# Local attention scores from a reordered key buffer: one product of 160 columns in place of products of 128 and 32

## The chip, the cores and the metric

The kernel runs on one core of a Trainium2 chip. A core has TensorE (PE in the profile, its weight loads are PEld), which multiplies matrices into PSUM; VectorE (DVE), ScalarE (ACT) and GpSimd (POOL), which work on elements; SyncE (SP), which here only issues DMAs; and 16 DMA engines. Each engine runs its own instructions in order and waits on semaphores for the others. The metric is the device time of one execution in microseconds (us), the median of several runs.

## The reference

The first half is attention with 32 global and 512 local tokens in each of 8 batches and 8 heads of 64 dimensions. The second half, a routed layer of eight experts over the 4352 tokens that come out, is not touched by the change.

```python
s_g = scale * np.matmul(q_g, k_all.transpose(0, 1, 3, 2))          # global queries, all keys
out_g = np.matmul(sm(s_g), v_all)
s_ll = scale * np.matmul(q_l, k_l.transpose(0, 1, 3, 2))
mask = np.abs(pos[:, None] - pos[None, :]) <= window               # window = 32
s_ll = np.where(mask, s_ll, -1000000000.0)
s_lg = scale * np.matmul(q_l, k_g.transpose(0, 1, 3, 2))           # local queries, global keys
out_l = np.matmul(sm(np.concatenate([s_lg, s_ll], axis=-1)), np.concatenate([v_g, v_l], axis=2))
```

So a local query sees the 32 global keys and the local keys at most 32 places away.

## The kernel before

**Tiling.** A unit n = 4b + hp is one batch b and one pair hp of heads; there are 32 units. The 512 local queries of a unit are cut into 8 blocks of 64. A block of both heads makes 128 rows; it needs 128 local keys (64 of its own, 32 on either side) and the 32 global ones, 160 scores in a row. Units 0 to 5 use a plainer form with the two heads in separate products (line 334); the change leaves that form alone.

**The loop** (lines 516 to 634) runs steps s = 0 to 33. The order of work on each engine is the order in which the program text issues it; nothing is rescheduled. Step s does, among other things:

- `st_B(s, 0..2)`: the scores of unit s in three parts of 3, 3 and 2 blocks. For each block, line 337 multiplies the queries `qbd` with 128 contiguous columns of the key buffer `kTe`, and line 339 multiplies the same queries with the 32 columns of `kgT`. VectorE then adds the mask and takes the maximum (L344), and ScalarE the exponentials into `Pu` (L347).
- `st_G1` in even steps: scores of the global queries of two units against all keys (L407), in rounds of four products, of 480, 32 and 32 columns; one call for each half g of a batch. `st_G2` and `st_G3` in odd steps finish them; the last product of `st_G3` (L433) reads `vgn`, the global values.
- `st_D1(s-1)`, `st_D2`: transposes of the exponentials (L354, L368) and of finished rows (L364), with their copies out of PSUM (L356, L370, L372).
- `st_A(s+1)`: transposes of the next unit's keys and queries (L305). VectorE copies the keys to `kTe` (L307), ScalarE the queries to `qbd` (L314, two copies).
- `st_E(s-1)`: the products with the values (L388). They read `va` and `vb` (local values in two alignments) and `vgz` (global values spread over the rows).
- from step 5 on, pieces of the first two experts fill the rest of TensorE's time: `p_l1` (L475, four products) and `p_l2` (L489, eight). They share two PSUM buffers, `ps_mm`, in turn, so a piece can start when the piece before last has been copied out: `p_l1` by ScalarE or VectorE (`hT`, L478 or L480), `p_l2` by ScalarE (`yst`, L492).

In a step the pieces come in the order p_l1, p_l2, p_l1, p_l1, p_l2, p_l1; where one step's last p_l1 is followed by the next step's first, the profile shows eight L475 in one row.

**Loads.** GpSimd issues the loads of q, k, v and of weights in its own order, through `queue`. SyncE issues `vgz` (L161) and `vgn` (L162) from a small DRAM copy `vg16`, and from batch 2 on three DMAs (L191 to L193) that move `va` into `vb`; in batches 0 and 1 GpSimd's copies do that (`part`). `clear_z` fills `vgz` and `vgn` once for each of their two buffers, on GpSimd. The results of `p_l2` are stored by SyncE, too (L496).

Of the kernel before, what the change touches and what calls it, by code (L numbers as in the profile page):

```python
# [18 lines left out]
NEG = -8.0e9  # L19
# [4 lines left out]
def kernel(  # L24
# [31 lines left out]
    KW = P  # L56
    SW = KW + Sg
    VW = Dh + 1
    assert (B, H, Sl, Dh, Sg) == (8, 8, 512, 64, 32) and D == H * Dh and F % P == 0
    scale = 1.0 / float(Dh) ** 0.5  # L60

# [66 lines left out]
    with ExitStack() as att:  # L128
# [5 lines left out]
        ps_po = att.enter_context(tc.tile_pool(name="ps_po", bufs=1, space=PSUM))  # L134

        qpl = [att_c.tile([P, Sl], FP16, name=f"qpl{i}") for i in range(2)]
        mask = att_c.tile([P, 3, SW], FP32)
        kgT = att_c.tile([P, HP, B * Sg], FP16)
        qgT = att_c.tile([P, HP, B * Sg], FP16)
        qbd = [att_c.tile([P, NHB, P], FP16, name=f"qbd{i}") for i in range(2)]  # L140
        kTe = [att_c.tile([P, W + Sl + W], FP16, name=f"kTe{i}") for i in range(4)]
        vgr = [att_c.tile([P, 4 * H * VW], FP16, name=f"vgz{i}") for i in range(2)]
        vgz = [t.rearrange("p (a h v) -> p a h v", a=4, h=H) for t in vgr]
        vgn = [att_c.tile([P, H, VW], FP16, name=f"vgn{i}") for i in range(2)]
        own = att_c.tile([P, 4], FP16)
# [13 lines left out]
        def load_vz(b):  # L159
            for i in range(4):  # L160
                nc.sync.dma_start(out=vgz[b % 2][i:P:4, i, :, 0:Dh], in_=vg16[b])  # L161
            nc.sync.dma_start(out=vgn[b % 2][P - Sg : P, :, 0:Dh], in_=vg16[b])  # L162

        def load_v(b):
            va, vb = vab[b % 2]
            vz = vgz[b % 2]
            src = v_l[b].rearrange("h s d -> s h d")

            def first():
                nc.gpsimd.dma_start(out=vg16[b], in_=v_g[b].rearrange("h g d -> g h d"))  # L170
                nc.gpsimd.dma_start(out=va[W:P, 0, :, 0:Dh], in_=src[0:96])

            def mid(j):
                nc.gpsimd.dma_start(out=va[:, j, :, 0:Dh], in_=src[P * j - W : P * j + 96])  # L174

            def last():
                nc.gpsimd.dma_start(out=vb[HB : HB + W, NJ - 1, :, 0:Dh], in_=src[Sl - W : Sl])

            def part(eng, lo):
                if lo:  # L180
                    eng.tensor_copy(out=vb[96:P, NJ - 1], in_=va[W : 2 * W, 0])
                    eng.tensor_copy(out=vb[0:HB, 0:2], in_=va[HB:P, 0:2])
                    eng.tensor_copy(out=vb[0:HB, 2:NJ], in_=va[HB:P, 2:NJ])
                else:
                    eng.tensor_copy(out=vb[HB:P, 0:2], in_=va[0:HB, 1:3])
                    eng.tensor_copy(out=vb[HB:P, 2], in_=va[0:HB, 3])

            def move():
                if b < 2:
# [4 lines left out]
                if b > 1:  # L194
                    load_vz(b)

            return [first] + [lambda j=j: mid(j) for j in range(1, NJ)] + [last, move]

# [61 lines left out]
        nc.scalar.activation(out=ones_f[:, 0:1], in_=ones_f[:, 0:1], func=AF.Exp, scale=0.0)  # L260
        nc.vector.memset(mask, 0.0)
        for t in (kTe[0], kTe[2], kTe[3]):
            nc.vector.memset(t[:, 0:W], 0.0)
            nc.vector.memset(t[:, W + Sl :], 0.0)

        def clear(i, eng):
            va, vb = vab[i]
# [22 lines left out]
        run(steps)  # L290
        clear_z(0, nc.gpsimd)
        load_vz(0)

        st = {}
        NPL = 6

        def st_A(n):
            b, hp = divmod(n, HP)
            qs, ks = staged[b]
            qb, kt = qbd[n % 2], kTe[n % 4]  # L300
            pt = [ps_tr.tile([P, Sl], FP16, tag="tr", name="pk"), ps_sc.tile([P, Sl], FP16, tag="sc", name="pq")]
            for t, src in enumerate((ks, qs)):
                for so in range(NJ):
                    for a in range(2):
                        nc.tensor.transpose(pt[t][HB * a : HB * (a + 1), P * so : P * (so + 1)],  # L305
                                            src[:, 2 * hp + a, so, :], identity)
            nc.vector.tensor_copy(out=kt[:, W : W + Sl].rearrange("c (p s) -> c p s", s=NJ),  # L307
                                  in_=pt[0].rearrange("c (s p) -> c p s", s=NJ))
            if n < NPL:
                nc.scalar.copy(out=qpl[n % 2].rearrange("c (p s) -> c p s", s=NJ), in_=pt[1].rearrange("c (s p) -> c p s", s=NJ))  # L310
                return
            for a in range(2):
                r = slice(HB * a, HB * (a + 1))
                nc.scalar.copy(out=qb[r, :, HB * a : HB * (a + 1)].rearrange("c i (p s) -> c i p s", s=NJ),  # L314
                               in_=pt[1][r].rearrange("c (s i p) -> c i p s", s=NJ, i=NHB))

        def st_B(n, part):
# [10 lines left out]
            for ii in range(ni):  # L328
                i = i0 + ii
                if n < NPL:  # L330
                    for c0, c1, kk in ((0, KW, kt[:, HB * i : HB * i + KW]), (KW, SW, kgT[:, hp, Sg * b : Sg * (b + 1)])):
                        for a in range(2):
                            r = slice(HB * a, HB * (a + 1))
                            nc.tensor.matmul(sc[r, SW * ii + c0 : SW * ii + c1], qpl[n % 2][r, HB * i : HB * (i + 1)],
                                             kk[r], start=True, stop=True)
                    continue
                nc.tensor.matmul(sc[:, SW * ii : SW * ii + KW], qb[:, i, :],  # L337
                                 kt[:, HB * i : HB * i + KW], start=True, stop=True)
                nc.tensor.matmul(sc[:, SW * ii + KW : SW * (ii + 1)], qb[:, i, :],
                                 kgT[:, hp, Sg * b : Sg * (b + 1)], start=True, stop=True)  # L340
            for ii in range(ni):
                i = i0 + ii
                mi = 0 if i == 0 else (2 if i == NHB - 1 else 1)
# [54 lines left out]
        def st_G1(b, g):  # L398
            n0 = HP * b + 2 * g
            gc = slice(Sg * b, Sg * (b + 1))  # L400
            sg = ps_po.tile([P, 2 * 512], FP32, tag="po")
            for c0, c1, k0 in ((0, Sl - W, 2 * W), (Sl - W, Sl, W), (Sl, S, None)):
                for hh in range(4):
                    pr, a = divmod(hh, 2)
                    r = slice(HB * a, HB * (a + 1))
                    rhs = kgT[r, 2 * g + pr, gc] if k0 is None else kTe[(n0 + pr) % 4][r, k0 : k0 + c1 - c0]
                    nc.tensor.matmul(sg[W * hh : W * (hh + 1), c0:c1], qgT[r, 2 * g + pr, gc], rhs, start=True, stop=True)  # L407
            m2 = att_wk.tile([P, 2], FP32, tag="m2")
            nc.vector.reduce_max(out=m2[:, 0:1], in_=sg[:, 0:S], axis=AX.X)
# [15 lines left out]
        def st_G3(b, g):  # L425
# [3 lines left out]
            for t in range(5):  # L429
                for par in range(2):  # L430
                    r, h0 = slice(HB * par, HB * (par + 1)), 4 * g + 2 * par
                    rhs = vb[:, t, h0 : h0 + 2, :] if t < NJ else vgn[b % 2][:, h0 : h0 + 2, :]
# [657 lines left out]
```

## Time and profile before

| what | value |
|---|---|
| median of 3 runs | 998.58 us (998.53 to 999.15) |
| the profiled execution's own time | 998.93 us |
| its span, first to last instruction | 997.2 us |
| granted TensorE clock over the span | 0.998 |
| TensorE busy | 982.5 us (99%) |
| VectorE busy | 767.2 us (77%) |
| ScalarE busy | 655.5 us (66%) |
| GpSimd busy | 301.7 us (30%) |
| line 337, 208 products of 128 columns | 27.6 us busy, 217 ns each |
| line 339, 208 products of 32 columns | 24.5 us busy, 178 ns each |
| line 307, 32 key copies on VectorE | 22.0 us busy, 687 ns each |
| line 314, 52 query copies on ScalarE | 32.5 us busy, 624 ns each |

The durations of products overlap, since a product starts while earlier ones still drain; so 217 and 178 ns are not what a product costs when others follow, and start times have to be compared instead. A line of the timeline gives the start, the duration, the engine, the line of the kernel, the operation, output and inputs, their shapes and how many instructions were merged; in brackets stands the idle time before it and what ended it. "Columns" of a product are those of its moving operand.

### The profile page before, as it was taken

Reading aid. Unit: us, or ns where it says so; the run is one execution under the profiler, and the core shown is the slowest. Engines: PE = TensorE matmul, PEld = TensorE weight load, DVE = VectorE, ACT = ScalarE, POOL = GpSimd, SP = SyncE. Lnnn points to the kernel's source line nnn. Section 1 sums busy time; section 2 is a strip of 40 time slices with the busy share of each in tenths; the row PEclk is TensorE's granted clock in tenths of the full one; section 3 lists DMA queues with packets and bytes.
Section 4 is the critical chain, followed back from the end, with each engine's and each line's share of the span. In section 5 each row is a group of like instructions: output and inputs, shape, how many; then the busy total and the mean of one; then the engine's idle time right before and its main releaser. Section 6 shows DMA issues by size and latency. Waiting matters only on the chain.

```text
span 997.2 us, 22451 instructions
## 1 busy us (share of the span) xinstructions
PE 982.5 (99%) x8868; PEld 641.0 (64%) x8868; DVE 767.2 (77%) x1858; ACT 655.5 (66%) x1342; POOL 301.7 (30%) x364
## 2 busy tenths in 40 slices
PE   7899999999999999999999999999999999999998
PEld 4566566656665555666666666676767676776764
DVE  7866665666653755889999888997899999888885
ACT  6888888888884566765555555557765555555551
POOL 9748887888850102111111111111111111100000
PEclk9999999999999999999999999999999999999999
DMA  9999999999952387554543333575664543123043
GB/s 167 186 156 199 239 206 221 222 200 222 234 144 85 108 241 169 161 147 121 122 107 74 75 75 74 128 214 129 165 148 117 117 96 66 53 65 74 2 106 127
DMA packets 138058, 138.68 MB, mean 139 GB/s; under 512 B 56608, under 2 KB 110048, under 8 KB 135904
## 3 DMA queue, kind: packets, MB, share of 16 engines
q0 software_dynamic: 105696, 87.32, 49.6%
q1 hardware_dynamic: 31696, 49.60, 15.5%
q8 instruction: 69, 1.13, 0.5%
q10 hardware_dynamic: 560, 0.33, 0.1%
q14 instruction: 37, 0.30, 0.1%
HBM read 144.46 MB, written 39.58 MB: 185 GB/s over the span
## 4 chain that ended last, share of the span: by engine, by line
PE 94%; POOL 3%; DMA 1%; DVE 1%; issue 0%; SPq 0%; ACT 0%; POOLq 0%; DVEq 0%
PE z L810 30%; PE pa L908 18%; PE py L489 12%; PE ph L475 12%; PE pb L908 9%; PE pc L908 4%; PE po L388 1%; PE ptw L354 1%; PE zp L879 1%; PE sc L337 1%; DMA vgz<-vg 1%; PE pk L305 1%; PE tgx L364 1%; PE pq L305 1%; PE sg L407 0%; POOL va L174 0%
## 5 line engine op out<-in xcount | busy, mean ns | idle before, releaser
L810 PEld LDWEIGHTS <-hs 128*128 128x128 f16 x2264 | 220.7, 98 | 91.8 <-DVE hs L806 0.4
L810 PE MATMUL z<-w2e,hs 128*128 128x256 f16 x1304 | 195.6, 273 | 0.0
L810 PE MATMUL z<-v,hs 128*128 128x256 f16 x960 | 144.0, 273 | 0.0
L475 PE MATMUL ph<-xT,w1e 128*128 128x512 f16 (+1 forms) x576 | 129.3, 367 | 0.6 <-ACT xT L372 0.6
L347 ACT ACTIVATE Pu<-ms,mx 128x160 f16<-128x160 f32 x256 | 120.1, 636 | 13.3 <-DVE mx L344 10.4
L489 PE MATMUL py<-w2e,hT 128*128 128x512 f16 x544 | 128.2, 379 | 0.0
L831 ACT COPY z<-z 128x256 f32<-128x256 f32 x98 | 35.0, 357 | 141.7 <-PE z L810 141.7
L908 PEld LDWEIGHTS <-w1e 128*128 128x128 f16 x960 | 87.1, 98 | 51.6 <-issue 1.0
L908 PE MATMUL pa<-t,s 128*128 128x512 f16 x384 | 114.2, 379 | 0.0
L726 POOL DMA_DIRECT2D w1e<-in_moe_w_dram x24 | 17.5, 734 | 297.5 <-PE pa L908 220.4
L344 DVE CUSTOM_DVE_ANT_0 ms<-sc,mask 128x160 f32<-128x160 f32 x256 | 70.2, 320 | 46.6 <-ACT yst L492 30.0
L844 DVE SCALAR_TENSOR_TENSOR oy<-z,lg,oy 128x512 f32<-128x512 f32 x128 | 95.8, 749 | 7.6 <-ACT oy L849 5.1
L806 DVE TENSOR_TENSOR hs<-hs 128x512 f16<-128x512 f16 x224 | 94.9, 424 | 8.2
L912 DVE CUSTOM_DVE_ANT_0 hx<-pb,s 128x512 f16<-128x512 f32 x96 | 65.9, 687 | 36.4 <-ACT s L942 30.2
L726 POOL DMA_DIRECT2D w2e<-in_moe_w_dram x24 | 19.8, 833 | 243.6 <-PE z L810 214.2
L928 ACT ACTIVATE hs<-pa 128x512 f16<-128x512 f32 x96 | 57.2, 596 | 47.0 <-PE pa L908 46.9
L475 PEld LDWEIGHTS <-w1e 128*128 128x128 f16 x576 | 53.4, 98 | 52.9
L912 DVE CUSTOM_DVE_ANT_0 hs<-pb,s 128x512 f16<-128x512 f32 x96 | 65.9, 686 | 24.1 <-ACT s L942 23.7
L908 PEld LDWEIGHTS <-s 128*128 128x128 f16 x720 | 65.6, 98 | 28.5 <-issue 0.3
L489 PEld LDWEIGHTS <-hT 128*128 128x128 f16 x544 | 49.8, 98 | 51.9
L480 DVE TENSOR_SCALAR hT<-ph 128x512 f16<-128x512 f32 x58 | 40.1, 692 | 55.1 <-PE ph L475 55.0
L478 ACT ACTIVATE hT<-ph 128x512 f16<-128x512 f32 (+1 forms) x86 | 50.6, 588 | 28.8 <-PE ph L475 28.4
(197 smaller groups left out, 1971.0 us busy)
## 6 DMA issues: line engine op xcount, KB each, us to landing
ys<-yd SPq DMA_DIRECT2D x68, 256.0 KB, 3.2
yd<-yst SPq DMA_DIRECT2D x16, 1024.0 KB, 5.9
pw<-in_moe_w_dram POOLq DMA_DIRECT2D x24, 512.0 KB, 10.1
kept<-psum POOLq DMA_DIRECT2D x24, 512.0 KB, 5.3
s<-kept POOLq DMA_DIRECT2D x12, 768.0 KB, 8.9
v<-kept POOLq DMA_DIRECT2D x12, 768.0 KB, 8.9
w1e<-in_moe_w_dram POOLq DMA_DIRECT2D x12, 512.0 KB, 5.3
w2e<-in_moe_w_dram POOLq DMA_DIRECT2D x12, 512.0 KB, 6.7
```

What stands on the lines that cost most here:

```text
L344: nc.vector.tensor_tensor_reduce(out=ms[:, ii, :], in0=sc[:, SW * ii : SW * (ii + 1)], in1=mask[:, mi, :], scale=-scale, scalar=BIG, op0=A ...
L347: nc.scalar.activation(out=d["Pu"][:, i // 4, :, i % 4], in_=ms[:, ii, :], func=AF.Exp, scale=-1.0, bias=d["mx"][:, i : i + 1])
L475: nc.tensor.matmul(ph[:, 0:n], wts[e][0][:, dk, P * fm : P * (fm + 1)], xT[:, dk, c0 : c0 + n], start=(dk == 0), stop=(dk == DP - 1))
L478: nc.scalar.activation(out=hT[:, fm, 0:n], in_=ph[:, 0:n], func=AF.Relu)
L480: nc.vector.tensor_scalar(out=hT[:, fm, 0:n], in0=ph[:, 0:n], scalar1=0.0, scalar2=None, op0=ALU.max)
L489: nc.tensor.matmul(py, hT[:, fk, P * c : P * (c + 1)], wts[e][1][:, fk, :], start=(fk == 0), stop=(fk == FT - 1))
L806: nc.vector.tensor_tensor(out=o, in0=x, in1=y, op=op)
L810: nc.tensor.matmul(o, lhs[:, fk, :], rhs[:, fk, :], start=(first and fk == 0), stop=(fk == HF - 1), skip_group_check=True)
L844: nc.vector.scalar_tensor_tensor(out=o, in0=z, scalar=p, in1=o, op0=ALU.mult, op1=ALU.add)
L908: nc.tensor.matmul(o, lhs[:, dk, P * f : P * (f + 1)], rhs[:, dk], start=(first and n == 0 and dk == 0), stop=(dk == HD - 1), skip_group_c ...
L912: nc.vector._custom_dve(TENSOR_ADD_SAT, out=self.to(i, j), in0=self.of(ps), in1=self.of(s), s0=BIG, s1=0.0)
L928: nc.scalar.activation(out=self.to(1, 0), in_=self.of(self.pa), func=AF.Relu)
```

## The change

It gives each key buffer `kTe` 24 pieces of 32 columns in place of 18. From unit 6 on, the keys lie in them in an order in which every fifth piece from piece 8 on holds the 32 global keys, written by a new ScalarE copy (`k_global`), and the local pieces lie such that each block's 160 keys can be read in one go: an odd block reads 160 contiguous columns, an even one five pieces of 32 that lie 64 columns apart. So the two products of a block become one. The copy of the local keys by VectorE becomes three copies.

In an odd block the keys then stand in another order, pieces 0, 2, 1, 3 as it were. From batch 2 on, the values `vb` are laid out in the same order (five moves by SyncE in place of three, the same bytes) and two permuted masks are made, in step 7. In batch 1 (`natural`), whose `vb` GpSimd fills in the old order, odd blocks keep two products and read the local keys through a permuted access pattern. `st_G1` reads its local keys in one round of 512 columns from batch 2 on, and in four of 128 in batch 1's second half.

`vgn` gets one buffer in place of two. Its load leaves `load_vz`: batch 0's stands behind the first `load_vz`, the others are issued at the start of step 4b + 2. GpSimd's fills of the second buffer go. A small tile of the routing part, `dg`, takes a buffer of the tag `ms`.

```diff
+    KC = 24
-        mask = att_c.tile([P, 3, SW], FP32)
+        mask = att_c.tile([P, 4, SW], FP32)
-        kTe = [att_c.tile([P, W + Sl + W], FP16, name=f"kTe{i}") for i in range(4)]
+        kTe = [att_c.tile([P, KC * W], FP16, name=f"kTe{i}") for i in range(4)]
-        vgn = [att_c.tile([P, H, VW], FP16, name=f"vgn{i}") for i in range(2)]
+        vgn = att_c.tile([P, H, VW], FP16)
+        def natural(b):
+            return b < 2
+        def k_block(n, i):
+            kt, r = kTe[n % 4], i // 2 * 5 * W
+            if i % 2:
+                return kt[:, r + 4 * W : r + 9 * W]
+            return kt[:, r : r + 9 * W].rearrange("c (k w) -> c k w", w=W)[:, 0:9:2]
+        def k_natural(n, i):
+            r = (i // 2 * 5 + 4) * W
+            return kTe[n % 4][:, r : r + 4 * W].rearrange("c (y x w) -> c x y w", x=2, w=W)
+        def k_global(n):
+            b, hp = divmod(n, HP)
+            kg = kTe[n % 4][:, 4 * W : 24 * W].rearrange("c (r k w) -> c r k w", k=5, w=W)[:, :, 4]
+            nc.scalar.copy(out=kg, in_=kgT[:, hp, Sg * b : Sg * (b + 1)].unsqueeze(1).to_broadcast([P, NJ, Sg]))
...
-            nc.sync.dma_start(out=vgn[b % 2][P - Sg : P, :, 0:Dh], in_=vg16[b])
...
-                nc.sync.dma_start(out=vb[0:HB, :], in_=va[HB:P, :])
-                nc.sync.dma_start(out=vb[HB:P, 0 : NJ - 1], in_=va[0:HB, 1:NJ])
+                nc.sync.dma_start(out=vb[0:W, :], in_=va[HB : HB + W, :])
+                nc.sync.dma_start(out=vb[HB : HB + W, :], in_=va[HB + W : P, :])
+                nc.sync.dma_start(out=vb[W:HB, 0 : NJ - 1], in_=va[0:W, 1:NJ])
+                nc.sync.dma_start(out=vb[HB + W : P, 0 : NJ - 1], in_=va[W:HB, 1:NJ])
...
-            eng.memset(vgn[i][0 : P - Sg], 0.0)
-            eng.memset(vgn[i][P - Sg : P, :, Dh:VW], 1.0)
+            if i == 0:
+                eng.memset(vgn[0 : P - Sg], 0.0)
+                eng.memset(vgn[P - Sg : P, :, Dh:VW], 1.0)
...
@@ st_A, from unit 6 on @@
+            ko = pt[0].rearrange("c (s r h o p) -> c o r h p s", s=NJ, r=4, h=2, o=2)
+            for o in range(2):
+                kd = kt[:, (2 + 2 * o) * W : (22 + 2 * o) * W].rearrange("c (r k p s) -> c r k p s", r=4, k=5, s=NJ)
+                kd = kd[:, :, 0:2] if o else kd[:, :, 0:5:4]
+                nc.vector.tensor_copy(out=kd, in_=ko[:, o])
+            nc.vector.tensor_copy(out=kt[:, 22 * W : 23 * W].rearrange("c (p s) -> c p s", s=NJ), in_=ko[:, 0, 0, 0])
+            k_global(n)
...
@@ st_B @@
-                nc.tensor.matmul(sc[:, SW * ii : SW * ii + KW], qb[:, i, :],
-                                 kt[:, HB * i : HB * i + KW], start=True, stop=True)
-                nc.tensor.matmul(sc[:, SW * ii + KW : SW * (ii + 1)], qb[:, i, :],
-                                 kgT[:, hp, Sg * b : Sg * (b + 1)], start=True, stop=True)
+                elif natural(b) and i % 2:
+                    nc.tensor.matmul(sc[:, SW * ii : SW * ii + KW], qb[:, i, :], k_natural(n, i), start=True, stop=True)
+                    nc.tensor.matmul(sc[:, SW * ii + KW : SW * (ii + 1)], qb[:, i, :],
+                                     kgT[:, hp, Sg * b : Sg * (b + 1)], start=True, stop=True)
+                else:
+                    nc.tensor.matmul(sc[:, SW * ii : SW * (ii + 1)], qb[:, i, :], k_block(n, i), start=True, stop=True)
...
@@ st_G1 @@
-            for c0, c1, k0 in ((0, Sl - W, 2 * W), (Sl - W, Sl, W), (Sl, S, None)):
+            if n0 < NPL:
+                cols = [(0, Sl - W, 2 * W), (Sl - W, Sl, W)]
+            elif natural(b):
+                cols = [(P * t, P * (t + 1), 2 * t + 1) for t in range(NJ)]
+            else:
+                cols = [(0, Sl, None)]
+            for c0, c1, k0 in cols + [(Sl, S, None)]:
...
+        def permuted_masks():
+            for i in (3, 2):
+                nc.vector.tensor_copy(out=mask[:, i, 0:KW].rearrange("q (y x w) -> q x y w", x=2, w=W),
+                                      in_=mask[:, 1, 0:KW].rearrange("q (x y w) -> q x y w", x=2, w=W))
+            nc.vector.memset(mask[:, 2, 3 * W : KW], NEG)
...
+            if 4 < s < NU and hp == 2:
+                nc.sync.dma_start(out=vgn[P - Sg : P, :, 0:Dh], in_=vg16[b])
...
+            if s == 7:
+                permuted_masks()
...
-            dg = att_wk.tile([P, P], FP32, tag="dg", bufs=1)
+            dg = att_wk.tile([P, 3, SW], FP32, tag="ms", name="dg")[:, 0, 0:P]
```

The masks are made behind `st_G3n` of step 7 and ahead of that step's last `p_l1`, whose copy out of PSUM is VectorE's (L480).

More of the change, by code (lines that the diff above doesn't have):

```diff
@@ L176, in last @@
             def last():
-                nc.gpsimd.dma_start(out=vb[HB : HB + W, NJ - 1, :, 0:Dh], in_=src[Sl - W : Sl])
+                r = HB if natural(b) else W
+                nc.gpsimd.dma_start(out=vb[r : r + W, NJ - 1, :, 0:Dh], in_=src[Sl - W : Sl])
             def part(eng, lo):
@@ L188, in move @@
             def move():
-                if b < 2:
+                if natural(b):
                     return part
                 nc.sync.dma_start(out=vb[96:P, NJ - 1], in_=va[W : 2 * W, 0])
-                nc.sync.dma_start(out=vb[0:HB, :], in_=va[HB:P, :])
-                nc.sync.dma_start(out=vb[HB:P, 0 : NJ - 1], in_=va[0:HB, 1:NJ])
-                if b > 1:
-                    load_vz(b)
+                nc.sync.dma_start(out=vb[0:W, :], in_=va[HB : HB + W, :])
+                nc.sync.dma_start(out=vb[HB : HB + W, :], in_=va[HB + W : P, :])
+                nc.sync.dma_start(out=vb[W:HB, 0 : NJ - 1], in_=va[0:W, 1:NJ])
+                nc.sync.dma_start(out=vb[HB + W : P, 0 : NJ - 1], in_=va[W:HB, 1:NJ])
+                load_vz(b)
             return [first] + [lambda j=j: mid(j) for j in range(1, NJ)] + [last, move]
@@ L262 @@
         for t in (kTe[0], kTe[2], kTe[3]):
-            nc.vector.memset(t[:, 0:W], 0.0)
-            nc.vector.memset(t[:, W + Sl :], 0.0)
+            nc.vector.memset(t[:, 0 : W], 0.0)
+            nc.vector.memset(t[:, W + Sl : 2 * W + Sl], 0.0)
         def clear(i, eng):
@@ L292 @@
         load_vz(0)
+        nc.sync.dma_start(out=vgn[P - Sg : P, :, 0:Dh], in_=vg16[0])
         st = {}
@@ L306, in st_A @@
                                             src[:, 2 * hp + a, so, :], identity)
-            nc.vector.tensor_copy(out=kt[:, W : W + Sl].rearrange("c (p s) -> c p s", s=NJ),
-                                  in_=pt[0].rearrange("c (s p) -> c p s", s=NJ))
+            kp = kt[:, W : W + Sl].rearrange("c (p s) -> c p s", s=NJ)
             if n < NPL:
+                nc.vector.tensor_copy(out=kp, in_=pt[0].rearrange("c (s p) -> c p s", s=NJ))
                 nc.scalar.copy(out=qpl[n % 2].rearrange("c (p s) -> c p s", s=NJ), in_=pt[1].rearrange("c (s p) -> c p s", s=NJ))
                 return
+            ko = pt[0].rearrange("c (s r h o p) -> c o r h p s", s=NJ, r=4, h=2, o=2)
[5 more added lines that the diff above has]
+            k_global(n)
             for a in range(2):
@@ L335, in st_B @@
                                              kk[r], start=True, stop=True)
-                    continue
-                nc.tensor.matmul(sc[:, SW * ii : SW * ii + KW], qb[:, i, :],
-                                 kt[:, HB * i : HB * i + KW], start=True, stop=True)
-                nc.tensor.matmul(sc[:, SW * ii + KW : SW * (ii + 1)], qb[:, i, :],
-                                 kgT[:, hp, Sg * b : Sg * (b + 1)], start=True, stop=True)
+                elif natural(b) and i % 2:
[4 more added lines that the diff above has]
+                    nc.tensor.matmul(sc[:, SW * ii : SW * (ii + 1)], qb[:, i, :], k_block(n, i), start=True, stop=True)
             for ii in range(ni):
                 i = i0 + ii
-                mi = 0 if i == 0 else (2 if i == NHB - 1 else 1)
+                mi = (0 if i == 0 else 2 if i == NHB - 1 else 1) if i % 2 == 0 or natural(b) else 2 if i == NHB - 1 else 3
                 nc.vector.tensor_tensor_reduce(
@@ L401, in st_G1 @@
             sg = ps_po.tile([P, 2 * 512], FP32, tag="po")
-            for c0, c1, k0 in ((0, Sl - W, 2 * W), (Sl - W, Sl, W), (Sl, S, None)):
+            if n0 < NPL:
[5 more added lines that the diff above has]
+            for c0, c1, k0 in cols + [(Sl, S, None)]:
                 for hh in range(4):
                     pr, a = divmod(hh, 2)
-                    r = slice(HB * a, HB * (a + 1))
-                    rhs = kgT[r, 2 * g + pr, gc] if k0 is None else kTe[(n0 + pr) % 4][r, k0 : k0 + c1 - c0]
+                    n, r = n0 + pr, slice(HB * a, HB * (a + 1))
+                    if c0 == Sl:
+                        rhs = kgT[r, 2 * g + pr, gc]
+                    elif n < NPL:
+                        rhs = kTe[n % 4][r, k0 : k0 + c1 - c0]
+                    elif natural(b):
+                        rhs = k_natural(n, k0)[r]
+                    else:
+                        rhs = kTe[n % 4][r, 4 * W : 24 * W].rearrange("c (t k) -> c t k", t=NJ)[:, :, 0:P]
                     nc.tensor.matmul(sg[W * hh : W * (hh + 1), c0:c1], qgT[r, 2 * g + pr, gc], rhs, start=True, stop=True)
@@ L431, in st_G3 @@
                     r, h0 = slice(HB * par, HB * (par + 1)), 4 * g + 2 * par
-                    rhs = vb[:, t, h0 : h0 + 2, :] if t < NJ else vgn[b % 2][:, h0 : h0 + 2, :]
+                    rhs = vb[:, t, h0 : h0 + 2, :] if t < NJ else vgn[:, h0 : h0 + 2, :]
                     nc.tensor.matmul(po[r, 0 : 2 * VW], pgs[:, t, r], rhs, start=(t == 0), stop=(t == 4))
```

## The prediction

> **What bounds the kernel now.** I read first the page's chain of work that ended last and then the busy time by stage.
>
> ```profile
> PE 94%; POOL 3%; DMA 1%; DVE 1%; issue 0%; SPq 0%; ACT 0%; POOLq 0%; DVEq 0%
> ...
> 60.00:305.00 245.00, 245.00 (x3081) 148.10 (x3080) 152.84 (x601) 205.48 (x435) 182.01 (x190) 1.00 1.05 207
> ```
>
> The second line is a stretch of the view by windows: TensorE's busy time comes right after the length, VectorE (152.84) and ScalarE (205.48) follow two columns on. From 60 to 305 us, the steps 8 to 32 of the attention loop, TensorE is busy all 245.00 us, and no wait of it is listed there. Busy shares can hide short waits, so I went through the start times of TensorE's instructions: in this stretch no kind of transition is ever over 0.1 us longer than its usual value. So a nanosecond taken from TensorE here is a nanosecond of the kernel, until another engine is late; before 55 us the chain runs through VectorE and transfers.
>
> **1. Scores.** The timeline of one score part (three blocks), TensorE alone:
>
> ```profile
> 182.42 0.22 PE L337 MATMUL sc<-kTe,qbd 128*128 128x128 f16 x1
> 182.47 0.18 PE L339 MATMUL sc<-kgT,qbd 128*128 128x32 f16 x1
> 182.50 0.22 PE L337 MATMUL sc<-kTe,qbd 128*128 128x128 f16 x1
> 182.56 0.18 PE L339 MATMUL sc<-kgT,qbd 128*128 128x32 f16 x1
> 182.58 0.22 PE L337 MATMUL sc<-kTe,qbd 128*128 128x128 f16 x1
> 182.64 0.18 PE L339 MATMUL sc<-kgT,qbd 128*128 128x32 f16 x1
> 182.74 0.40 PE L407 MATMUL sg<-kTe,qgT 64*32 64x480 f16 x8
> ...
> 111.83 0.44 PE L420 MATMUL pt<-identity,Pg 128*128 128x128 f16 x5
> ...
> 107.67 1.90 PE L489 MATMUL py<-w2e,hT 128*128 128x512 f16 x8
> ```
>
> What counts is start to start: wide to narrow 55 ns, narrow to the next wide 28, so 83 a block; 26 to another product of the full array; but 107 to one that uses part of it (L407, L305 or L388). A product of 160 is not in the trace. 128 columns take (0.44 - 0.22) / 4 = 55 ns (L420) and 512 take (1.90 - 0.38) / 7 = 217 (L489), so 0.42 ns a column and 69 for 160. Before a partial product, the spacing is 107 after 32 columns, 152 after 130 (L433 to L489) and 309 after 512 (L475 to L407), so 160 after 160.
> Units 8 to 31 have 24 x 8 = 192 blocks, all in the full stretch: 120 are followed by a block, 36 by a full product, 36 by a partial one. Before: 120 x 83 + 36 x 81 + 36 x 162 = 18.7 us. After: 156 x 69 + 36 x 160 = 16.5 us. **Saved 2.2 us**; eight merged blocks of units 6 and 7 add 0.03, most of them lying ahead of other waits.
> A rule of the Trainium skill would make this far larger: "TensorE: Matmul & The Clock Gate", section "Back-to-back issue gap", gives about 81 ns for each 128-column product that has its own weight load. By it the pair would cost about 162 ns and the single product about 90, an estimate of 14 us saved; the trace disagrees, with 55.
> **2. Global queries' scores.** A round of L407 with 480 columns takes 203 ns, one with 32 takes 28; one of 512 takes 216. 12 calls x 15 ns = 0.18 us saved. The call of batch 1's second half has four rounds of 56 in place of 231: nothing.
>
> **3. VectorE's key copy** becomes three (256, 256 and 32 elements) from unit 6 on. L307 holds the queue 0.60 us (58.14 to 58.74 below). Durations go from 189 ns for 32 elements (L464) to 687 for 512, 1.04 ns an element; with the same 0.08 overlap the three hold it 0.34 + 0.34 + 0.10, **+0.18 us**. The next hT copy (L480) covers that: it sits idle 0.69 to 1.31 us waiting for TensorE in steps 9 to 31, 0.33 in step 8, 0.37 in step 6, 1.23 in step 5. Not in step 7:
>
> ```profile
> 58.14 0.69 DVE L307 COPY kTe<-pk 128x512 f16<-128x512 f16 x1
> 58.74 0.20 DVE L392 RECIPROCAL rr<-po 128x8 f32<-128x8 f32 x1
> ...
> 59.77 0.57 DVE L446 TENSOR_SCALAR xgn<-pog,rg 32x64 f16<-32x64 f32 x2
> 60.37 0.69 DVE L480 TENSOR_SCALAR hT<-ph 128x512 f16<-128x512 f32 x1
> ...
> 61.34 0.38 PE L489 MATMUL py<-w2e,hT 128*128 128x512 f16 x1
> ```
>
> L480 follows L446 at once, and L489 takes the PSUM buffer that L480 empties, 0.28 us after its end (61.06). **4. The permuted masks** go exactly there: two copies of 128 and a fill, in front of L480. Their like at the start (L509 4.84, L510 4.98, L511 5.33, next at 5.44) held VectorE 0.6 us; I take 0.55. So L480 comes 0.18 + 0.55 = 0.73 later, less 0.28 of room that the 0.05 of a signal narrows: TensorE waits **0.5 us** once (0.3 to 0.8). Queued behind it are the three L344 of step 8 and the exps they feed, which run without a pause from 61.7 to 68.6; 0.1 for that (0 to 0.3).
>
> **5. ScalarE's copy of the global keys** into the buffer stands ahead of the two L314 of each step from 5 on. It moves 128 elements; L370 (256) holds the queue 0.26 us until L372, an L347 of 160 holds it 0.36. I take 0.18 (0.1 to 0.3), nearest to L370 in kind. What is queued behind:
>
> ```profile
> 108.27 1.28 ACT L314 COPY qbd<-pq 64x512 f16<-64x512 f16 x2
> 109.61 0.59 ACT L492 COPY yst<-py 128x512 f32<-128x512 f32 x1
> ...
> 109.41 1.89 PE L475 MATMUL ph<-xT,w1e 128*128 128x512 f16 x8
> ```
>
> L492 empties the buffer that the fifth of these eight L475 writes, at 110.27; L492 ends at 110.20. With 0.05 for the signal that leaves 0.03, and L492 itself started 0.03 after ScalarE could have. In odd steps L492 idles 0.33 before it, and in steps 10, 14 ... 30 and 8 the buffer is needed 0.48 us or more after it: covered. In steps **12, 16, 20, 24 and 28** nothing covers it: 5 x (0.18 - 0.06) = **0.6 us** lost (0.2 to 1.2).
>
> **6. Moved at no cost.** SP issues five vb moves for three at about 0.6 us each and one vgn load by itself. The tightest user is batch 2: its last vgz lands at 72.73, its first L388 is at 76.34; 1.2 to 2 us later still fits, and if not it costs about 1. vgn is issued at the start of step 4b+2; vgn loads land in 4.3 to 10.9 us and the user comes in the step after, over 15 us on; its wait is for a product of the step before, so yd stores queued behind it lose nothing. Pool drops two fills (0.74 us) in step 2, which does not bring the wait for vgz at 42.17 forward: SP had waited until 30.01 for vg itself. VectorE's longer fills at the start (480 to 640 elements, 288 to 384) add some 0.25 us ahead of L281, which waits 0.34 for its DMA. The last stage has TensorE busy 653.03 of 657.20 us and carries the shift on.
>
> **Sum.** -2.2 - 0.2 + 0.5 + 0.1 + 0.6 = -1.2 us. The profiled execution has a span of 997.2 and a time of 998.93; it becomes 997.7. The median of the runs, 998.58, is 0.35 below, so I predict **997.4**. About 0.2% (2.0 us) is what a measurement can tell from no change.
>
> **Rivals.** *Covers hold* (0.20): ScalarE's copy runs in the shadow of its neighbours and the masks take 0.25: 2.4 us less some 0.2 stay, 996.4. For it: L314 already starts 0.25 us before the last L347 ends. Against: room of only 0.06.
> *Runs of 32 read slowly* (0.14, slower): even blocks take their 160 columns as five runs of 32, 24 x 4 = 96 products. Against: L908 reads its 512 in two runs of 256 and still starts every 216 ns. For: loading weights at every fourth element (L354) takes 113 ns in place of 98. Fifteen per 128 is 19 for 160, 1.8 us in all: 999.2. At half speed it is 96 x 69 = 6.6 us: 1004. It decides from 12 ns a product on (1.2 / 96). The Trainium skill, "Advanced Engine Details and Errata", section "Memory Cachelines", says that two hits in a 16-byte line are enough; 32 halves fill four lines, so by it this rival is void. L354's starts of 56 ns agree, though no run here shows a moving operand in such runs.
> *Late vgz of batch 2* (0.07): 998.4. *Each product paid with its load* (0.02): were starts at least a weight load apart, 98 ns in the rows, 192 loads would go, 18.8 us in place of 2.2: 981. The 55 ns speak against it. The Trainium skill's "TensorE: Matmul & The Clock Gate", section "Back-to-back issue gap", points to that side.
>
> **How the numbers follow.** Forecast 0.55 (996.7 to 998.2); 0.02 for stalls beyond the bounds. Faster: 0.20 + 0.02 + 0.03 of the forecast's edge = 0.25. Slower: 0.10 of the slow reading's 0.14, the 0.02 and 0.01 of late vgz = 0.13. The rest is 0.62. The range, 996.0 to 999.6, takes in no stall at all and the small form of slow reading.
>
> **What would show it.** Products of 160 at starts of 69 ns, even and odd alike; one wait of about 0.5 us before the first py of step 8, ended by L480's successor; waits of about 0.1 in steps 12, 16 ... 28 at the fifth product behind py, ended by the yst copy; no other wait between 60 and 305 us. Wrong would be: even blocks slower than odd ones, waits in odd steps, or an end of the loop not some 1.2 us earlier.

## The result and the profile after

| | before | after |
|---|---|---|
| median of 22 runs | 999.35 us (997.97 to 1001.55) | 997.43 us (996.23 to 1000.06) |
| ratio after / before, 95% interval | | 0.9983 [0.9977, 0.9990] |
| the profiled execution: time, span | 998.93, 997.2 us | 996.94, 995.2 us |

By the ratio the change gains 1.7 us (0.0017 x 999.35; 1.0 to 2.3 by the interval); the two medians differ by 1.9. 997.4 was forecast. Line numbers are now those of the changed kernel (in the kernels of the experiments some lie up to four further on): the block's product is L370, the global-key copy L168, the three key copies L338 (two) and L339, the query copies L343, the mask copies L559 and the fill L561; `hT` is copied out by L521 (ScalarE) and L523 (VectorE), `p_l1` is L518, `p_l2` L532, its copy out L535.

The page's chain of work after, and from the view by windows the stretch that the prediction shows (length, busy time of TensorE, its weight loads, VectorE, ScalarE, GpSimd; then clock, DMA share, GB/s):

```profile
PE 95%; DVE 2%; ACT 2%; DMA 0%; issue 0%; SPq 0%; DVEq 0%; ACTq 0%
...
60.00:305.00 245.00, 244.56 (x2856) 143.08 (x2849) 157.26 (x648) 209.62 (x459) 181.04 (x189) 1.00 1.07 208
```

TensorE has 0.44 us of idle time in this stretch, where it had none. The rest of the new waits is hidden inside "busy", because a product that starts late lies behind one that still drains.

The timeline of TensorE after, a score part of three blocks, then the global round:

```profile
181.54 0.37 PE L370 MATMUL sc<-kTe,qbd 128*128 128x160 f16 x3
181.84 0.40 PE L450 MATMUL sg<-kTe,qgT 64*32 64x512 f16 x4
182.07 0.19 PE L450 MATMUL sg<-kgT,qgT 64*32 64x32 f16 x4
182.19 0.64 PE L384 MATMUL ptw<-identity,Pu 128*128 128x128 f16 x8
```

Three products of 0.233 us fill 0.37, so they start (0.37 - 0.233) / 2 = 69 ns apart; the partial product follows 0.30 after the first, that is 2 x 69 and 162. Over units 8 to 31 the starts are 69 or 70 ns apart for even and odd blocks alike (one of 80 apart) and 162 to 163 before a partial product. Forecast were 69 and 160.

The trace puts the difference of the two profiled executions in these places. The stretch runs from the first value product (L388, now L418) of unit 6 to that of unit 31:

| stretch | before | after | difference |
|---|---|---|---|
| start to unit 6 | 57.56 | 56.84 | -0.72 |
| unit 6 to unit 31 | 250.78 | 249.81 | **-0.96** |
| unit 31 to TensorE's last instruction | 685.24 | 685.21 | -0.02 |
| from there to the end of the span | 3.58 | 3.31 | -0.28 |

The second row is steady: in six traces whose loop has the products and copies of the kernel before (experiment 7 has the other five) it is 250.75 to 250.78 us. The forecast's terms all lie in this row, and it had -1.2 there. Summed by start-to-start times, the row holds: scores -2.04 (18.69 to 16.65), global rounds -0.15, two waits before L532 in step 8 +0.50 and +0.18, five waits at the fifth L518 +0.53 (0.10 to 0.11 each), one at the first score product of step 8 +0.08, and -0.06 of small things.

There are two main kinds of waits. The first is in step 8; VectorE, ScalarE and the products that wait:

```profile
58.32 1.18 ACT L343 COPY qbd<-pq 64x512 f16<-64x512 f16 x2
...
59.23 0.56 DVE L489 TENSOR_SCALAR xgn<-pog,rg 32x64 f16<-32x64 f32 x2
59.55 0.18 PEld L370 LDWEIGHTS <-qbd 128*128 128x128 f16 x3 [0.41 <-ACT qbd L343]
...
59.82 0.62 DVE L559 COPY mask<-mask 128x128 f32<-128x128 f32 x2
59.88 0.63 ACT L492 ACTIVATE xgn<-pog,rg 32x64 f16<-32x64 f32 x2 [0.39 <-DVE xgn L489]
...
60.51 0.09 DVE L561 MEMSET mask<- 128x32 f32 x1
60.54 0.60 ACT L521 ACTIVATE hT<-ph 128x512 f16<-128x512 f32 x1
60.63 0.69 DVE L523 TENSOR_SCALAR hT<-ph 128x512 f16<-128x512 f32 x1
...
61.19 0.81 PE L532 MATMUL py<-w2e,hT 128*128 128x512 f16 x3 [0.33 <-ACT hT L521]
```

L523 starts at 60.63, 0.84 after the end of L489 (59.79); before, L480 followed L446 by 0.03. But L532 starts at 61.19, while L523 still runs (to 61.32): what it waits for is L521, which ends at 61.13. The 0.08 is in the row of L370: its weights wait for the query copies, which ScalarE's new copy has put off, and the product starts 300 ns behind an L518 instead of 216.

The second kind, here at the end of step 12:

```profile
107.86 0.36 ACT L168 COPY kTe<-kgT 128x128 f16<-128x128 f16 x1
108.13 1.17 ACT L343 COPY qbd<-pq 64x512 f16<-64x512 f16 x2
108.99 1.77 PE L518 MATMUL ph<-xT,w1e 128*128 128x512 f16 x7
109.32 0.58 ACT L535 COPY yst<-py 128x512 f32<-128x512 f32 x1
```

L168 holds ScalarE's queue for 0.26 us (107.86 to 108.13), L535 comes right behind L343 and ends at 109.905, and the fifth L518 starts at 109.96, 319 ns behind the fourth instead of 216. Behind the copies of steps 16, 20, 24 and 28 it is 318, 320, 324 and 329. (The row counts seven of the eight products because the window ends at 110.4.) The waiting time does not show in the merged row at all; only start times tell it.

### The profile page after: what moved, and what is told of

Same layout as the page of the kernel before. It is cut to its first block, busy times and chain, and to the rows that moved or that the text cites. A ratio compares the mean times of both kernels' runs of the same rounds, so it can differ in the third digit from the quotient of the medians.

```text
span 995.2 us, 22059 instructions
## 1 busy us (share of the span) xinstructions
PE 981.3 (99%) x8628; PEld 635.7 (64%) x8628; DVE 772.9 (78%) x1913; ACT 659.1 (66%) x1368; POOL 300.3 (30%) x362
## 4 chain that ended last, share of the span: by engine, by line
PE 95%; DVE 2%; ACT 2%; DMA 0%; issue 0%; SPq 0%; DVEq 0%; ACTq 0%
PE z L863 30%; PE pa L961 18%; PE py L532 12%; PE ph L518 11%; PE pb L961 9%; PE pc L961 4%; PE ptw L384 1%; PE po L418 1%; PE sc L370 1%; PE zp L932 1%; ACT Pu L377 1%; PE pk L327 1%; PE tgx L394 1%; DVE ms L374 1%; PE pq L327 1%; DMA f<-in_k_g_dram 0%
## 5 line engine op out<-in xcount | busy, mean ns | idle before, releaser
L518 PE MATMUL ph<-xT,w1e 128*128 128x512 f16 (+1 forms) x576 | 129.8, 367 | 0.6 <-ACT xT L402 0.6
L532 PE MATMUL py<-w2e,hT 128*128 128x512 f16 x544 | 128.2, 379 | 0.4 <-ACT hT L521 0.3
L377 ACT ACTIVATE Pu<-ms,mx 128x160 f16<-128x160 f32 x256 | 120.2, 636 | 12.5 <-DVE mx L374 10.4
L518 PEld LDWEIGHTS <-w1e 128*128 128x128 f16 x576 | 54.6, 98 | 53.4 <-issue 1.1
L532 PEld LDWEIGHTS <-hT 128*128 128x128 f16 x544 | 49.9, 98 | 52.4 <-issue 0.5
L523 DVE TENSOR_SCALAR hT<-ph 128x512 f16<-128x512 f32 x58 | 40.1, 691 | 51.5 <-PE ph L518 51.5
L521 ACT ACTIVATE hT<-ph 128x512 f16<-128x512 f32 (+1 forms) x86 | 50.7, 590 | 27.7 <-PE ph L518 27.2
```

What stands on the lines that cost most here:

```text
L377: nc.scalar.activation(out=d["Pu"][:, i // 4, :, i % 4], in_=ms[:, ii, :], func=AF.Exp, scale=-1.0, bias=d["mx"][:, i : i + 1])
L518: nc.tensor.matmul(ph[:, 0:n], wts[e][0][:, dk, P * fm : P * (fm + 1)], xT[:, dk, c0 : c0 + n], start=(dk == 0), stop=(dk == DP - 1))
L521: nc.scalar.activation(out=hT[:, fm, 0:n], in_=ph[:, 0:n], func=AF.Relu)
L523: nc.vector.tensor_scalar(out=hT[:, fm, 0:n], in0=ph[:, 0:n], scalar1=0.0, scalar2=None, op0=ALU.max)
L532: nc.tensor.matmul(py, hT[:, fk, P * c : P * (c + 1)], wts[e][1][:, fk, :], start=(fk == 0), stop=(fk == FT - 1))
```

## The experiments

**1. The masks elsewhere.** Mask 3 made in step 5, mask 2 in step 8 ahead of its third `p_l1`.

```diff
-            if s == 7:
-                permuted_masks()
+            if s == 5:
+                permuted_mask(3)
+            if s == 8:
+                permuted_mask(2)
```

> The changed kernel with the permuted masks made elsewhere: mask 3 ahead of the third p_l1 of step 5, mask 2 ahead of the third p_l1 of step 8, where VectorE sits idle 1.2 and 0.8 us. In the changed kernel TensorE waits 0.50 us before the first py of step 8 and 0.18 before the second. My theory (the masks delay the copy that empties the PSUM buffer): both waits go down to 0.1 at most, the waits of 0.11 in steps 12, 16 ... 28 stay, the loop ends 0.5 to 0.7 us earlier, about 996.9 us against 997.4. Rival (the wait comes from the three key copies, or from which of the two buffers py gets): at least 0.3 of the wait stays.

One run took 996.73 us. The stretch takes 249.19 us, 0.62 less than in the changed kernel. Both waits before L532 in step 8 are gone, and the five at the fifth L518 stay (0.11 to 0.12 each). Its step 8:

```profile
59.60 0.56 DVE L489 TENSOR_SCALAR xgn<-pog,rg 32x64 f16<-32x64 f32 x2
60.20 0.69 DVE L523 TENSOR_SCALAR hT<-ph 128x512 f16<-128x512 f32 x1
60.26 0.63 ACT L492 ACTIVATE xgn<-pog,rg 32x64 f16<-32x64 f32 x2 [0.38 <-DVE xgn L489]
60.92 0.60 ACT L521 ACTIVATE hT<-ph 128x512 f16<-128x512 f32 x1
...
61.07 0.81 PE L532 MATMUL py<-w2e,hT 128*128 128x512 f16 x3
```

L532 starts while L521 still runs (to 61.51), so it now uses the buffer that L523 emptied at 60.89. So the masks cost both waits, 0.68 us. They do it by a path that my theory did not have; it is the one that the rival named (which buffer the product gets), though no 0.3 us stayed. The copy out of the other buffer, L521, ends too late for this product in every trace (0.44 behind its start here). In the five traces with the masks in step 7 (the change and experiments 2, 4, 6 and the fills of 7) L532 starts 0.05 behind L521's end; with the masks elsewhere (here, experiments 3 and 5) it takes the buffer of VectorE, which had been ready for 0.18 here. In two of the five, experiment 2 and the fills, L523 had ended 0.07 ahead of L521, and L532 still started 0.05 behind L521; so which copy ends first does not decide it, and the buffer is taken to be settled in the program. Why the program with the masks in step 7 has the other buffer, no run shows.

**2. The global-key copy on VectorE.**

```diff
-            nc.scalar.copy(out=kg, in_=...)
+            nc.vector.tensor_copy(out=kg, in_=...)
```

> The changed kernel with the copy of the global keys into the buffer made by VectorE, behind its key copies, in place of ScalarE. My theory (ScalarE's copy delays the yst copy in the steps where it has no room): the five waits of 0.11 us in steps 12, 16, 20, 24 and 28 go, nothing new comes since VectorE waits 0.56 us or more for TensorE behind its key copies; the loop ends 0.5 to 0.6 us earlier. The wait in step 8 stays. Rival (those waits come from TensorE arriving earlier, by the faster scores): they stay at 0.05 or more each.

One run took 997.85 us, its stretch 249.38, 0.43 less than the changed kernel's. The five waits are gone, and so is the 0.08 of step 8: they came from ScalarE's copy. The first wait before L532 in step 8 grew from 0.50 to 0.70, the second is gone, and one of 0.14 came in step 30. The copy takes 183 to 189 ns in 17 of 26 cases, as a short copy should, but 429 to 1839 in nine.

**3. Both together.**

> The changed kernel with both: masks made in steps 5 and 8, the copy of the global keys on VectorE. My theory: the waits of both kinds go and the two gains add up, 1.0 to 1.2 us under the changed kernel, so about 996.3 us where the kernel before takes 999.35; no wait of TensorE over 0.1 us between 60 and 305 us. Rival (VectorE becomes late somewhere with both jobs, above all in step 8): a new wait of 0.2 us or more, and less than 0.8 us gained.

The median of 12 runs is 997.47 us, ratio 0.9981 [0.9966, 0.9995], no better than the change itself; the rival holds. The stretch takes 249.77. The waits of experiments 1 and 2 are gone but for 0.07 and 0.10 us in step 8; 1.06 us came back in step 24 (0.38 at L450, 0.58 at L532, 0.10 at the second L532), through one VectorE copy at the end of step 23:

```profile
218.73 2.78 DVE L168 COPY kTe<-kgT 128x128 f16<-128x128 f16 x1
219.09 2.35 POOL L121 TENSOR_TENSOR psum<-pw 128x512 f16<-128x512 f16 x2
...
221.66 0.69 DVE L423 TENSOR_TENSOR xn<-po,rr 128x512 f16<-128x512 f32 x1
...
222.40 0.40 PE L450 MATMUL sg<-kTe,qgT 64*32 64x512 f16 x4 [0.31 <-DVE xn L423]
```

The copy of 188 ns stands for 2779 and ends at 221.508, 64 ns after GpSimd's L121 pair (221.444). In the two runs, 20 of the 21 copies that took over 200 ns end so: 48 to 64 ns behind an L121, or 19 to 25 behind a DMA issue of GpSimd's. In all 21 a GpSimd instruction had begun before the copy. So a VectorE copy from SBUF to SBUF can wait for GpSimd here. It does not always: 18 of the other 31 copies overlap a GpSimd instruction, too, 17 of them DMA issues alone, and take 183 to 191 ns. The Trainium skill, "SBUF — State Buffer", section "Who interferes with whom", says that VectorE in a two-port mode, which a copy can enter, contends with GpSimd for a pair of ports that whoever issued first holds for its whole instruction. The 21 long copies agree as far as GpSimd had begun first; the one shown here was also passed over by both L121, which began behind it. In which mode a copy ran, no trace shows.

**4. All of the change but the single product.** Two products per block, the same bytes copied.

```diff
-    nc.tensor.matmul(sc[:, SW * ii : SW * (ii + 1)], qb[:, i, :], k_block(n, i), start=True, stop=True)
+    kb = k_block(n, i)
+    nc.tensor.matmul(sc[:, SW * ii : SW * ii + KW], qb[:, i, :], kb[:, 0:KW] if i % 2 else kb[:, 0:4], start=True, stop=True)
+    nc.tensor.matmul(sc[:, SW * ii + KW : SW * (ii + 1)], qb[:, i, :], kgT[:, hp, Sg * b : Sg * (b + 1)], start=True, stop=True)
```

> The changed kernel with two products per block again (128 columns from the reordered buffer, 32 from kgT); all else of the change stays, the copy of the global keys too, which nothing reads then. My theory: merging alone is worth 2.2 us, so the loop ends 2.2 us later than in the changed kernel and the time is 999.4 to 999.8, at or a little over the kernel before. Even blocks, read in runs of 32, start their narrow product 55 ns after the wide one, as odd blocks do. Rival (the gain lies in the start of the kernel, not in the products): less than 1.5 us is lost against the changed kernel.

The median of 10 runs is 999.56 us, ratio 1.000 [0.9987, 1.0012]. The stretch takes 251.71, 0.93 more than before and 1.89 more than with the single product; its score products take 18.71 us against 16.65. So the merge alone is worth 2.06 us, and the rest of the change costs 0.93 in the loop. That the stretch grew by less than 2.06 is because the added waits are shorter here (0.47 and 0.11 before L532 in step 8, 0.09 each at the fifth product).

**5. No stalls.** Experiment 1, and in even steps ScalarE's copy issued behind `yst`, where ScalarE is idle.

```diff
-            k_global(n)
+            if n < 9 or n % 2 == 0:
+                k_global(n)
...
             f2("a")
+            if 8 <= s < NU and s % 2 == 0:
+                k_global(s + 1)
```

> The changed kernel with mask 3 made in step 5 and mask 2 in step 8 (as in the run with the masks spread), and with ScalarE's copy of the global keys in even steps from 8 on issued behind the yst copy of the same step, where ScalarE then idles 1.1 us, in place of ahead of the two query copies. Theory (every loss of the change is a late copy out of PSUM): neither the 0.50 and 0.18 us waits of step 8 nor the five of 0.113 us are left, no new one appears, and from the first value product of unit 6 to that of unit 30 the kernel takes 249.81 - 0.68 - 0.56 = 248.6 us; the median goes to about 996.2. Rival (TensorE has a second limit right behind): the waits return elsewhere in the same steps, the stretch stays over 249.2 us, the median is 997.0 or more.

(The stretch meant there is the one of the table; it ends with unit 31, not 30.) The median of 12 runs is **996.35 us**, ratio 0.9974 [0.9961, 0.9987]. The stretch takes 248.65 us (248.6 expected); of the waits only the 0.08 of step 8 is left, whose copy was not moved, and TensorE is busy all 245.00. Step 12 and the windows row:

```profile
109.08 1.89 PE L519 MATMUL ph<-xT,w1e 128*128 128x512 f16 x8
109.28 0.58 ACT L536 COPY yst<-py 128x512 f32<-128x512 f32 x1
109.76 0.30 ACT L168 COPY kTe<-kgT 128x128 f16<-128x128 f16 x1
...
111.00 0.60 ACT L522 ACTIVATE hT<-ph 128x512 f16<-128x512 f32 x1 [0.94 <-PE ph L519]
```

```profile
60.00:305.00 245.00, 245.00 (x2863) 143.58 (x2862) 157.68 (x649) 210.71 (x461) 181.66 (x190) 1.00 1.11 208
```

Eight L519 now take 1.89 us, as before the change, and ScalarE still has 0.94 us to spare behind the copy. The rival, a second limit right behind, is out: taking away 1.21 us of waits (0.50, 0.18 and 0.53) made the stretch 1.16 shorter. That rests on the traces; the ratios of this kernel and of the change have intervals that overlap.

**6. ScalarE's copy twice** from unit 9 on.

```diff
             k_global(n)
+            if n > 8:
+                k_global(n)
```

> The changed kernel with ScalarE's copy of the global keys issued twice from unit 9 on (the second writes the same again). Theory (the copy costs what it holds ScalarE's queue, 0.26 us, less the room behind it): the five waits in steps 12, 16, 20, 24 and 28 go from 0.113 to 0.37 us; in odd steps 9 to 29 the yst copy idles 0.17 before it and its buffer is needed 0.08 after its end, of which a signal takes 0.05, so eleven new waits of 0.07 us; in steps 10, 14, 18, 22, 26 and 30, with 0.34 behind the copy, none. Together 1.3 + 0.8 = 2.1 us over the changed kernel, about 999.5. Rival (the copy is absorbed, the 0.113 has another cause): the waits stay at 0.11, under 0.3 us in all. Second rival (ScalarE is a bound in every step): 24 times 0.26, 6.2 us.

The median of 10 runs is 1000.77 us, ratio 1.0015 [1.0004, 1.0027]. The stretch takes 253.25, 3.44 more than the changed kernel's, not 2.1. Step 12:

```profile
108.87 0.68 ACT L168 COPY kTe<-kgT 128x128 f16<-128x128 f16 x2
109.46 1.17 ACT L345 COPY qbd<-pq 64x512 f16<-64x512 f16 x2
110.65 0.58 ACT L537 COPY yst<-py 128x512 f32<-128x512 f32 x1
111.28 0.59 PE L520 MATMUL ph<-xT,w1e 128*128 128x512 f16 x2 [0.26 <-ACT yst L537]
```

The two copies hold 0.59 us (108.87 to 109.46), so the second adds 0.33, not 0.26: it writes the same place and starts only 31 or 32 ns after the first has ended. With 0.33 the steps come out as the theory has them: 0.42 to 0.43 in the five tight steps (0.11 + 0.32) and 0.15 in the eleven odd ones (0.33 less 0.17 idle and 0.02 of room is 0.14), none in steps 10, 14 and their like. These make 3.2 of the 3.44. Both rivals (the waits stay as they were; 24 times 0.26) are out.

**7. Where the 0.7 us ahead of unit 6 come from.** Before, TensorE waits about 1 us for `vgz` in step 5. The view of waits, 39 to 44 us, of the kernel before has 0.8, since it counts from the end of the product in front; the table below goes by start times, which gives 0.16 more:

```profile
PE po L388 <- DMA vgz<-vg: 0.8, 1, 0.8
```

After, no such row is there. Four kernels: the kernel before run again, twice; the kernel before with the values part alone (one `vgn`, its loads by themselves, no second fills), twice; the same with the larger buffers and their fills; and the changed kernel with GpSimd fills of that size put back.

```diff
+            if i == 1:
+                eng.memset(vgr[1][0 : P - Sg, 0 : H * VW], 0.0)
+                eng.memset(vgr[1][P - Sg : P, 0:H], 0.0)
```

> The kernel before with one part of the change alone: one vgn buffer, its loads issued by themselves, GpSimd's two fills of the second buffer gone. Theory (nothing of this is on the path; the earlier start of the changed kernel's loop is scatter between executions): the first value product of unit 6 starts anywhere between 56.8 and 58.1 us, as in the six traces so far, and follows the landing of the fourth vgz load of batch 1, which scatters between 39.6 and 42.2 us. Rival (the fills and the load were what delayed vgz): the fourth load of batch 1 is issued before 32.0 us and lands before 40.0, no wait for vgz at 41 us, unit 6 at 56.9 or before.

> The kernel before, unchanged, for a second execution's trace. Theory (scatter at the start): the landing of batch 1's vgz loads and the start of unit 6's value products differ from the first trace (42.17 and 57.56 us) by several tenths. Rival (the start is fixed by the program): both within 0.1 us of the first trace, a wait of 1.0 us for vgz at 41.2 again.

> The kernel before with the values part of the change and, on top, the memory layout of the changed kernel: key buffers of 24 pieces and a mask of four planes with their longer fills at the start, and dg in a buffer of the tag ms; products and copies of the loop stay as before. From the issue of batch 1's first vgz load to the landing of the fourth it took 12.1 and 12.9 us in the two executions of the kernel before and 12.1 in the one with the values part alone, 8.8 to 11.9 in the seven with the rest of the change. Theory (scatter; the change does not decide it): this one can fall anywhere in 8.8 to 13. Rival (the layout or the fills of VectorE make the landing earlier): under 11.9, and no wait for vgz over 0.3 us.

> The changed kernel with GpSimd fills of the size of the two that the change dropped, ahead of the vgz fill of batch 1. Theory (the fills are not on the path): from the issue of the first vgz load to the landing of the fourth 8.8 to 11.9 us, as in the other seven traces with the change, and unit 6's value products start between 56.8 and 58.2. Rival (the fills held vgz back): first issue 0.7 us later, a wait for vgz of 0.5 to 1.0 us in step 5.

> The kernel before, unchanged, for a third trace of its start. Theory (scatter): the time from the first vgz issue of batch 1 to the landing of the fourth can come under 11.9 us, with a wait under 0.3. Rival (the program sets it): 12 to 13 us again and a wait for vgz of 0.6 to 1.0 us.

> The kernel before with the values part alone, a second trace of its start. Theory (scatter): the time from the first vgz issue of batch 1 to the landing of the fourth can come under 11.9 us. Rival (the program sets it): 12 to 13 us again and a wait for vgz of 0.6 to 1.0 us.

The four `vgz` loads of batch 1, from the first issue to the last landing, and the start of unit 6's value products:

| kernels | first issue to fourth landing | wait for vgz in step 5 | unit 6 starts |
|---|---|---|---|
| before (3 traces) | 12.1, 12.9, 12.4 | 0.96, 0.64, 1.02 | 57.56, 58.24, 58.06 |
| before + values part (2) | 12.1, 12.5 | 0.71, 0.47 | 58.66, 58.05 |
| + larger buffers and their fills (1) | 11.3 | 0.77 | 56.82 |
| the change and its variants (8, the one with fills included) | 8.8 to 11.9 | 0.27 in one, else 0 | 56.84 to 58.44 |

Their times were 999.61, 999.42 (before), 1000.02, 999.41 (values part), 998.20 (larger buffers) and 998.44 (fills back).

Neither the third trace of the kernel before nor the second of the values part came under 11.9, which scatter alone would have allowed, and two starts of unit 6 (58.66 and 58.44) lie outside what was expected. GpSimd's fills and the `vgn` load are not the cause: without them nothing comes earlier, and with fills put back the landing stays at 11.6. Pure scatter is hardly it either: the five traces without the larger buffers are all above 12, the nine with them all below. The single trace of the larger buffers alone points to the layout or VectorE's fills; which of the two, and how, is open, and its wait of 0.77 shows that one trace does not settle it. The start of unit 6 scatters by 1 us or more within each group; its mean goes from 58.1 (five traces) to 57.6 (eight), so the change may be worth about 0.5 us there, an estimate from few traces. The 0.28 at the end of the span goes with the change, too: 3.58 to 3.61 us in the six traces without it, 3.31 or 3.32 in the eight with it. The larger buffers alone do not bring it (3.61); its cause stays open.

## Why the prediction was right

The forecast held, 997.4 against 997.43, but that the two are so close is luck. It took 1.2 us off a median of three runs, 998.58; over 22 runs the kernel before has 999.35, 0.77 more. From there 1.2 us less would have been 998.2. So a base that was 0.77 too low and a gain that was 0.5 to 0.7 too small cancelled. The gain itself has two parts: the loop gave 0.96 instead of 1.2, and about 0.8 (the estimate of 0.5, and 0.28) came from places that I had priced at nothing. These sum to 1.7, well inside the interval of 1.0 to 2.3.

- **Scores.** 2.04 of 2.2. Before was right to 0.02 us (18.71 worked out, 18.69 measured); after came out 0.13 larger than the 16.52 worked out, from starts of 69.3 and 162.4 in place of 69 and 160. Experiment 4 shows that this saving comes from the merge.
- **Global queries.** 0.15 of 0.18; the 512-column rounds start 216 ns apart, as forecast.
- **Key copies.** They hold VectorE 0.77 us; forecast 0.78. Nothing waits for that outside step 8.
- **Masks.** The first wait is 0.50, as forecast, but this step had the wrong path: I had L480's successor end it, and L521 on ScalarE ends it. I had sized the masks at 0.55 us; here they take 0.84, since the second L559 ends at 60.437, 51 ns after GpSimd's DMA issue that began at 59.589 (60.386). In the run with fills back no such issue overlaps, the masks take 0.58, and the wait is still 0.50: the buffer of L521 sets it. So the size of the masks did not matter for this wait and the agreement on 0.5 is chance. The queue behind it cost 0.18, forecast 0.1 (0 to 0.3); in the run with fills back, with the shorter masks, that second wait is missing.
- **ScalarE's copy.** Five waits behind the copies of the steps named, 0.10 to 0.11 each against 0.12. The copy holds the queue 0.26 us, not 0.18, but the two L343 behind it take 1.17 us in place of 1.28, so the net delay, 0.15, was close to forecast. The 0.08 in step 8 was not foreseen. Experiments 5 and 6 confirm this account: room of 0.05 in those steps, 0.17 idle in odd ones, 0.34 behind the copy in steps 10, 14 and on.
- **Moved at no cost.** This step failed for the start. That dropping two fills "does not bring the wait for vgz at 42.17 forward" was right as it stood, yet the wait went with the change; by which of its other parts stays open.
- **Late vgz of batch 2.** No: it lands at 71.63, the first user is at 76.2.
- **The rivals.** *Runs of 32 read slowly*: no, even and odd blocks both start 69 ns apart; that agrees with the Trainium skill, "Advanced Engine Details and Errata", section "Memory Cachelines", by which two hits in a 16-byte line are enough. *Each product paid with its load*: no, 69 is under the 98 of a load. *Covers hold*: not in the change; the kernel without stalls is about what it would have been, 996.35 (996.4 named for it, from the same low base).

## What to carry to other kernels

Where one engine is busy all the time, price a change by start-to-start times, and then walk every buffer that this engine reuses: work added to another engine costs only where a copy out of that buffer has less room than the addition. If two engines empty such buffers, look at the room of both, since the program may turn to the other. Before adopting the change, move the added copies into idle time of their engines: that was worth 1.16 us of the loop, more than the change gained there by itself.

## What the runs showed of the hardware

- A VectorE copy inside SBUF of 183 to 191 ns took 242 to 2779 in 21 of 52 cases. Each time a GpSimd instruction was already under way, and the copy ended 19 to 64 ns behind a GpSimd instruction (one case apart), a DMA issue as well as an element operation. 18 others overlapped GpSimd, mostly its DMA issues, at their usual time. ScalarE's copy of the same data took 286 to 391 ns in the changed kernel, 354 to 362 in 23 of 26 cases.
- A moving operand in runs of 32 elements 64 columns apart costs nothing against a contiguous one: 69 ns for 160 columns at a granted clock of 1.00.
- A second ScalarE copy to the same place starts only 31 or 32 ns after the first has ended; two different copies overlap by about 0.1 us (L168 lasts 0.36 and holds 0.26).
